# Retention, softplus and SwiGLU feed-forwards in one kernel: retention chunks 4 to 11 taken two at a time, with another order of tiles, conversions and loads around them

## The chip, the cores and the metric

One core of a Trainium2 chip runs the whole program. The metric is the device time of one execution in microseconds, as the median of a few runs.

## What is computed

Three stages follow each other: a multi-head retention (a linear attention whose state decays by a factor per head), a feed-forward layer with softplus, and a feed-forward layer with RMS norm and SwiGLU. Inputs are float32, and the weights reach the kernel as 64-bit numbers, which it converts itself.

```python
B, H, S, D = 2, 8, 768, 64                      # retention
for t in range(S):
    state = gamma * state + einsum('bhd,bhe->bhde', k[:, :, t], v[:, :, t])
    y[:, :, t] = scale * einsum('bhd,bhde->bhe', q[:, :, t], state)
x = y.transpose(0, 2, 1, 3).reshape(1536, 512)
h = x @ w_in                                    # 512 -> 2048
x = softplus(h) @ w_out                         # 2048 -> 512
xn = x / sqrt(mean(x * x) + 1e-6) * rms_g
out = (silu(xn @ w_gate) * (xn @ w_val)) @ w_out2   # 512 -> 1536 -> 512
```

## The kernel before

**Retention in chunks.** The 768 positions of each of the two batch rows are cut into 6 chunks of 128, so there are 12 chunks, 0 to 11; four of them make one block of 512 tokens, the tile `x[bi]` (blocks 0 to 2). One chunk takes these steps on TensorE, each for all 8 heads:

- `step_t` (L250 to L270): eight transposes `pt` of k and q. VectorE multiplies the turned q by a decay table into the tile `at` (L261), ScalarE copies the turned k into it (L266). Both must be there before the scores.
- `step_s`: products `sc` of turned k and q (L278). VectorE multiplies them by the masks (L280, two instructions of 128x512).
- `step_u`: products `u` of k and v (L291); GpSimd has scaled k first (`prep`, L248). VectorE adds `u` to the faded state (L297); GpSimd fades the state (`fade`, L302). The last chunk of a batch row, 5 and 11, has no such step.
- `step_y`: products `y` of state and q (L318; not in the first chunk of a batch row, 0 and 6), then of v and the masked scores into the same banks (L325). ScalarE writes a rounded high part into `x[bi]`, VectorE the rest (`split`, L119).

These products use parts of TensorE's array: `sc` has tiles of 64x128, `y` from the state 64x64, `y` from v and `u` 128x64; the transposes and all large products use the whole 128x128. The profile prints that shape behind the names.

**Large products.** `project` (L342) makes one tile `h` of the first layer from 12 matmuls of 512 columns: four pieces of the contraction for each of three products of high and low parts. `l2` (L378) makes the tiles `l` in the same way. `l1`'s `after()` is the softplus: Abs, Exp and Ln on ScalarE (L359 to L361), one VectorE instruction (L362), and later a split into `g`.

**Weights.** `load_weight` brings a tile of 512 KB into one of three stages, `convert` makes the float32 high and low parts: ScalarE `c` and `a` (L163, L164), VectorE `w` twice (L165, L167), GpSimd the sum `c` (L169), and from the list `deferred` VectorE `a` (L178, `finish`), ScalarE the high part and GpSimd the low part (L120, L121). The order on VectorE is the order in which the code issues.

**Order.** The schedule is written by hand: every engine runs its instructions in the order of the code and waits on semaphores. Chunks 0 to 3 run first (L552). Then, while block 0 and block 1 of the first layer are computed, each `h` tile is followed by one chunk (L579 to L608): the chunk's `y` and `u`, the scores of the next chunk, and the transposes of the chunk after the next one. So a chunk's transposes, scores and outputs lie about one `h` tile (and more) apart. After that only large products follow to the end. All loads go through SyncE's queue in the order of the code; the eight PSUM banks are handed out in turn by `bank`.

Of the kernel before, what the change touches and what calls it, by code (L numbers as in the profile page):

```python
# [26 lines left out]
def retention_softplus_swiglu(ctx: ExitStack, tc: tile.TileContext, q, k, v, w_in, w_out,  # L27
# [31 lines left out]
    def bank(name, keep=False):  # L59
        i = oldest.pop(0)  # L60
        (kept if keep else oldest).append(i)
        return ps.tile([P, N], F32, tag=f"ps{i}", name=name)
# [91 lines left out]
    def convert():  # L154
        i = pos["conv"]
        if i >= pos["load"] or not free:
# [6 lines left out]
        nc.scalar.activation(out=c, in_=lo32, func=AF.Copy, scale=2.0 ** -29)  # L163
        nc.scalar.activation(out=a, in_=hi32.bitcast(F32), func=AF.Abs)  # L164
        nc.vector.tensor_scalar(out=w, in0=hi32, scalar1=3, scalar2=0x3FFFFFF8,  # L165
                                op0=ALU.logical_shift_left, op1=ALU.bitwise_and)
        nc.vector.scalar_tensor_tensor(out=w, in0=hi32, scalar=0xC0000000, in1=w,  # L167
                                       op0=ALU.bitwise_and, op1=ALU.bitwise_or)
        nc.gpsimd.tensor_tensor(out=c, in0=w, in1=c, op=ALU.add)  # L169
# [12 lines left out]

        deferred.append(finish if order[i][0] in ("w_in", "w_out") else lambda: deferred.append(finish))
        ws[order[i]] = t
        left[order[i]] = NB
        pos["conv"] += 1
        return True
# [11 lines left out]

    def flush(loads=True, order=1):  # L200
        todo = deferred[::order]
        deferred.clear()
        for s in todo:
            s()
        if loads:
            load_weight()
# [65 lines left out]
    def step_s(g):  # L272
# [6 lines left out]
        for e in range(2):  # L279
            nc.vector.tensor_tensor(out=t[:, 2 + e], in0=sc[e], in1=mask[e], op=ALU.mult)  # L280

    def step_u(g):
        c = g % CPB
        _, kk, vv = [qkv[g].pop(i) for i in range(3)]
        if c == CPB - 1:
            return
        u = bank("u")[:, 0:NP * D].rearrange("p (j t) -> p j t", j=NP)
        for j in range(NP):
            for e in range(2):
                h = 2 * j + e  # L290
                nc.tensor.matmul(u[e * D:(e + 1) * D, j, :], lhsT=kk[:, h, :], rhs=vv[:, NP * e + j, :],  # L291
                                 start=True, stop=True, skip_group_check=True)
        new = state[(c + 1) % 2]
        if c == 0:
            nc.vector.tensor_copy(new, u)
        else:
            nc.vector.tensor_tensor(out=new, in0=u, in1=faded, op=ALU.add)  # L297
# [7 lines left out]
    def step_y(g):  # L305
        c = g % CPB
        bi, ci = divmod(g, CB)
        if ci == 0:
            x[bi] = x_p.tile([P, 2, KC, N], F32R, tag="x", name=f"x{bi}")


        ys = [bank("y")[:, 0:2 * P].rearrange("p (i t) -> p i t", i=2) for _ in range(2)]
        t = tr.pop(g)

        if c:
            for i in range(2):
                for e, h in ((0, 0), (1, 1), (0, 1), (1, 0)):
                    nc.tensor.matmul(ys[e][h * D:(h + 1) * D, i, :], lhsT=state[c % 2][e * D:(e + 1) * D, 2 * i + h, :],  # L318
                                     rhs=t[e * D:(e + 1) * D, 0, 2 * i + h, :], start=(i == 0), stop=False,
                                     skip_group_check=True)  # L320
        for e in range(2):
            for i in range(2):
                for h in range(2):
                    j = 2 * i + h
                    nc.tensor.matmul(ys[e][h * D:(h + 1) * D, i, :], lhsT=qkv[g][2][:, NP * e + j, :], rhs=t[:, 2 + e, j, :],  # L325
                                     start=(c == 0 and i == 0), stop=True, skip_group_check=True)
        sl = slice(ci * P, (ci + 1) * P)
        for e in range(2):
            k2 = slice(2 * e, 2 * e + 2)
            split(x[bi][:, 0, k2, sl], x[bi][:, 1, k2, sl], ys[e])  # L330
# [22 lines left out]
    def l1(b, f):  # L353
        h = bank("h")
        project(h, weight("w_in", f), x[b])

        def after():
            t = t_p.tile([P, N], F32, tag="t", name="t")
            nc.scalar.activation(out=t, in_=h, func=AF.Abs)  # L359
# [3 lines left out]
            split_later((b, f), t)  # L363
        return after

    def l2(b, gr, m):
        fs = range(gr * G1, (gr + 1) * G1)
        keep = b == 0
        if keep:
            if gr == 0:  # L370
                acc[b, m] = bank("l2", True)
            p = acc[b, m]
        else:
            p = bank("l2")
# [106 lines left out]
    def l4(b, gr, m, fs=None):  # L481
# [3 lines left out]
        if fs[0] == grp[0]:  # L485
            if keep:
                if gr == 0:
                    acc["o", b, m] = bank("l4", True)
# [63 lines left out]
    for g in range(CB):  # L552
        load_next(g + 2)
        load_weight()
        if g == CB - 1:
            nc.sync.dma_start(out=rg, in_=rms_g.rearrange("(k p) -> p k", p=P))
        step_y(g)
        step_u(g)
        if g < CB - 1:
            fade(g)  # L560
        step_s(g + 1)
        if g < CB - 1:
# [3 lines left out]
        flush(False)  # L566
        if g % 2:
            convert()

    pend = None  # L570
    for gr in range(NG1):
        for b in range(NB):
            l1s = [lambda f=f: l1(b, f) for f in range(gr * G1, (gr + 1) * G1)]
# [3 lines left out]
            if pend:  # L577
                l2s = [lambda m=m: l2(*pend, m) for m in range(KC)]
# [100 lines left out]
```

## Time and profile before

| what | value |
|---|---|
| median of 3 runs | 621.01 us (620.82 to 622.0) |
| the profiled execution: its own time | 621.34 us |
| the profiled execution: span of its instructions | 619.6 us |
| TensorE busy (PE) | 613.1 us, 99% of the span |
| VectorE (DVE), ScalarE (ACT), GpSimd (POOL) busy | 382.4, 320.9, 197.9 us |
| granted TensorE clock | 1.00 of full speed (2.4 GHz) in every stretch |
| retention chunks lie within | the first 83.2 us |

The span is 1.7 us shorter than the execution's own time. Busy PE says little by itself, because matmuls are pipelined: how close together they start is read from the timeline.

### The profile page before, as it was taken

The page shows a single profiled execution, that of the slowest core. Times are in us where ns is not written, and L with a number is a line of the kernel's source. Part 1 is how long each engine was busy: PE and PEld are TensorE (multiplying, and loading weights), DVE is VectorE, ACT ScalarE, POOL GpSimd, SP SyncE. Part 2 cuts the span into 40 slices and gives each one's busy share as a digit, 9 for nine tenths or more (in the row PEclk, how much of TensorE's full clock was granted, in tenths as well). Part 3 has the DMA queues.
Part 4 walks back from the last instruction along what each step waited for, and adds up shares of the span by engine and source line. Part 5 has one row for each costly group of instructions (what it writes and reads, how often), then busy time and mean ns, then how long its engine had stood idle before and what let it go on. Part 6 is the DMA issues. An engine that isn't in the chain of part 4 may idle for free.

```text
span 619.6 us, 8589 instructions
## 1 busy us (share of the span) xinstructions
PE 613.1 (99%) x3304; PEld 509.4 (82%) x3304; DVE 382.4 (62%) x588; ACT 320.9 (52%) x555; POOL 197.9 (32%) x162
## 2 busy tenths in 40 slices
PE   9999999999999999999999999999999999999997
PEld 8788888888888888888888888888888888888885
DVE  5799817777754776367689866536683466722332
ACT  3477538887765776487576446324342334411111
POOL 3456404445520543033024425304252134400000
PEclk9999999999999999999999999999999999999999
DMA  9999312333220332021023313212231113000102
GB/s 198 238 246 226 86 35 68 103 102 103 71 66 1 102 103 68 1 71 66 0 69 103 93 45 102 69 34 69 68 104 34 49 54 103 0 1 18 51 35 102
DMA packets 65560, 48.84 MB, mean 79 GB/s; under 512 B 39792, under 2 KB 60528, under 8 KB 65520
## 3 DMA queue, kind: packets, MB, share of 16 engines
q1 hardware_dynamic: 64320, 47.90, 27.8%
q8 instruction: 26, 0.43, 0.3%
q10 hardware_dynamic: 1200, 0.39, 0.3%
q14 instruction: 14, 0.11, 0.1%
HBM read 45.14 MB, written 3.15 MB: 78 GB/s over the span
## 4 chain that ended last, share of the span: by engine, by line
PE 98%; DMA 1%; DVE 0%; ACT 0%; issue 0%; SPq 0%
PE l L378 21%; PE h L342 21%; PE l L496 16%; PE h_w_gate L342 16%; PE h_w_val L342 16%; PE sc L278 2%; PE y L325 2%; PE pt L259 2%; PE y L318 1%; PE u L291 1%; DMA k<-in_k_dram 1%; PE busy L212 0%; PE ms L433 0%; PE root L449 0%; DVE at L280 0%; PE pt L234 0%
## 5 line engine op out<-in xcount | busy, mean ns | idle before, releaser
L169 POOL TENSOR_TENSOR c<-w,c 128x512 uint32<-128x512 uint32 x68 | 87.9, 1292 | 243.8 <-DVE w L167 209.0
L342 PE MATMUL h<-x,ws_w_in 128*128 128x512 f32 x576 | 139.2, 391 | 0.0
L378 PE MATMUL l<-g,ws_w_out 128*128 128x512 f32 x576 | 137.9, 390 | 0.0
L378 PEld LDWEIGHTS l<-g,ws_w_out 128*128 128x128 f32 x576 | 107.9, 188 | 22.6 <-issue 0.2
L342 PEld LDWEIGHTS h<-x,ws_w_in 128*128 128x128 f32 x576 | 107.6, 188 | 22.2
L120 ACT ACTIVATE g<-t 128x512 fp32r<-128x512 f32 x84 | 53.1, 632 | 109.4 <-DVE t L477 79.3
L342 PE MATMUL h_w_gate<-xn,ws_w_gate 128*128 128x512 f32 x432 | 104.0, 390 | 0.0
L342 PE MATMUL h_w_val<-xn,ws_w_val 128*128 128x512 f32 x432 | 103.9, 389 | 0.0
L496 PE MATMUL l<-ws_w_out,g 128*128 128x512 f32 x432 | 103.4, 389 | 0.0
L496 PEld LDWEIGHTS l<-ws_w_out,g 128*128 128x128 f32 x432 | 81.0, 188 | 16.8
L342 PEld LDWEIGHTS h_w_val<-xn,ws_w_val 128*128 128x128 f32 x432 | 81.0, 188 | 16.8
L342 PEld LDWEIGHTS h_w_gate<-xn,ws_w_gate 128*128 128x128 f32 x432 | 80.9, 188 | 16.7
L362 DVE SCALAR_TENSOR_TENSOR t<-h,t 128x512 f32<-128x512 f32 x48 | 33.2, 691 | 79.3 <-ACT t L361 79.2
L121 DVE TENSOR_TENSOR g<-t,g 128x512 fp32r<-128x512 f32 x84 | 62.1, 739 | 25.1 <-ACT g L120 21.6
L473 ACT ACTIVATE t<-t 128x512 f32<-128x512 f32 x36 | 22.8, 633 | 90.2 <-DVE t L472 90.2
L477 DVE TENSOR_TENSOR t<-h_w_val,t 128x512 f32<-128x512 f32 x36 | 24.8, 689 | 63.0 <-PE h_w_val L342 61.7
L178 DVE SCALAR_TENSOR_TENSOR a<-a,c 128x512 f32<-128x512 f32 x68 | 59.7, 879 | 3.8 <-POOL c L169 3.8
L359 ACT ACTIVATE t<-h 128x512 f32<-128x512 f32 x48 | 28.7, 597 | 47.8 <-PE h L342 47.7
L121 POOL TENSOR_TENSOR ws_w_out<-a,ws_w_out 128x512 fp32r<-128x512 f32 x28 | 36.2, 1294 | 40.1 <-ACT ws_w_out L120 40.1
L472 DVE TENSOR_TENSOR t<-h_w_gate,root 128x512 f32<-128x512 f32 x36 | 24.8, 688 | 25.6 <-PE h_w_gate L342 23.7
L121 POOL TENSOR_TENSOR ws_w_in<-a,ws_w_in 128x512 fp32r<-128x512 f32 x16 | 22.7, 1416 | 36.9 <-ACT ws_w_in L120 36.9
L361 ACT ACTIVATE t<-t 128x512 f32<-128x512 f32 x48 | 30.4, 633 | 1.5
(88 smaller groups left out, 578.7 us busy)
## 6 DMA issues: line engine op xcount, KB each, us to landing
st_w_out<-in_moe_w_out_dram SPq DMA_DIRECT2D x28, 512.0 KB, 3.3
st_w_in<-in_moe_w_in_dram SPq DMA_DIRECT2D x16, 512.0 KB, 3.8
st_w_gate<-in_moe_w_gate_dram SPq DMA_DIRECT2D x12, 512.0 KB, 3.5
st_w_val<-in_moe_w_val_dram SPq DMA_DIRECT2D x12, 512.0 KB, 3.5
v<-in_v_dram SPq DMA_DIRECT2D x12, 256.0 KB, 4.8
q<-in_q_dram SPq DMA_DIRECT2D x23, 128.0 KB, 4.5
k<-in_k_dram SPq DMA_DIRECT2D x23, 128.0 KB, 4.2
out_dram<-o SPq DMA_DIRECT2D x11, 256.0 KB, 2.0
```

Source lines behind the costliest of these rows:

```text
L120: nc.scalar.activation(out=hi, in_=src, func=AF.Copy)
L121: eng.tensor_tensor(out=lo, in0=src, in1=hi.bitcast(F32), op=ALU.subtract)
L169: nc.gpsimd.tensor_tensor(out=c, in0=w, in1=c, op=ALU.add)
L178: nc.vector.scalar_tensor_tensor(out=a, in0=a, scalar=TINY, in1=c.bitcast(F32), op0=ALU.is_ge, op1=ALU.mult)
L342: nc.tensor.matmul(h, lhsT=w[:, i, kk * P:(kk + 1) * P], rhs=src[:, j, kk, :], start=(n == 0), stop=(n == 3 * KC - 1))
L359: nc.scalar.activation(out=t, in_=h, func=AF.Abs)
L361: nc.scalar.activation(out=t, in_=t, func=AF.Ln, bias=1.0)
L362: nc.vector.scalar_tensor_tensor(out=t, in0=h, scalar=0.0, in1=t, op0=ALU.max, op1=ALU.add)
L378: nc.tensor.matmul(p, lhsT=w[:, i, m * P:(m + 1) * P], rhs=g_t[b, f][:, j, :], start=(n == 0 and f == (0 if keep else fs[0])), stop=(n == ...
L472: nc.vector.tensor_tensor(out=t, in0=h, in1=root[b], op=ALU.mult)
L477: nc.vector.tensor_tensor(out=t, in0=h, in1=t, op=ALU.mult)
L496: nc.tensor.matmul(p, lhsT=g_t[b, f][:, j, m * P:(m + 1) * P], rhs=w[:, i, :], start=(n == 0 and f == (0 if keep else grp[0])), stop=(n == ...
```

## The change

Chunks 4 to 11 are taken as the pairs (4, 5), (6, 7), (8, 9), (10, 11) in a new function `batch`. In a pair the transposes of both chunks stand together, then all scores, all `u`, the products from the state, and the products from v. `u` of both chunks shares one bank, and so do the two chunks' `y` (each split is now one instruction of 512 elements where there were two of 256). The steps of `convert` are issued apart from each other within the pair. Between the pairs stand one or two `h` tiles: one before (4, 5) and (6, 7), two before (8, 9) and (10, 11). The loads and conversions of the region are written out by hand.

```diff
+    def outputs(gs):
...
+        w = len(gs) * P
+        ys = [bank("y")[:, 0:2 * w].rearrange("p (i t) -> p i t", i=2) for _ in range(2)]
...
+        for n, g in enumerate(gs):
+            c = g % CPB
+            if c:
+                for i in range(2):
+                    for e, h in ((0, 0), (1, 1), (0, 1), (1, 0)):
+                        product(e, h, i, n, state[c % 2][e * D:(e + 1) * D, 2 * i + h, :],
+                                tr[g][e * D:(e + 1) * D, 0, 2 * i + h, :], False)
+        for n, g in enumerate(gs):
+            for e in range(2):
+                for i in range(2):
+                    for h in range(2):
+                        j = 2 * i + h
+                        product(e, h, i, n, qkv[g][2][:, NP * e + j, :], tr[g][:, 2 + e, j, :], True)
...
+    def batch(a, after, more=()):
+        gs = (a, a + 1)
+        after.size()
+        rest = take()
+        parts = convert(True)
+        if parts:
+            bits, small, total, size, finish = parts
+            bits()
+        if a not in tr:
+            step_t(a)
+        if parts:
+            small()
+        step_t(a + 1)
+        for g in gs:
+            prep(g)
+        if parts:
+            total()
+        scores(a)()
+        masked = scores(a + 1)
+        after()
+        if parts:
+            size()
+        adds = update(gs)
+        if adds:
+            adds.pop(0)()
+            fade(a)
+        masked()
+        parted = outputs(gs)
+        if adds:
+            adds.pop(0)()
+        todo = take()
+        for do in rest:
+            do()
+        if parts:
+            finish()
+        for do in todo:
+            do()
+        for do in take():
+            do()
+        parted()
...
+            elif (gr, b) == (0, 1):
+                after = first[0]()
...
+                batch(4, after)
...
+                batch(6, first[1]())
+                load(8, 2)
+                load(9, 2)
+                load_weight()
+                load(10, 0)
+                load(10, 1)
+                convert()
+                load_weight()
+                load(11, 0)
+                load(11, 1)
+                piece(first[2](), 1)
+                batch(8, l1s[0]())
+                load(10, 2)
+                load(11, 2)
+                piece(first[3](), 1)
+                batch(10, l1s[1]())
+                piece(l1s[2](), 0)
+                piece(l2s.pop(0)(), 0)
```

`bits` are the two VectorE instructions `w`, `small` and `size` the ScalarE ones, `total` GpSimd's sum, `finish` the VectorE instruction `a` with the splits behind it.

TensorE, one full chunk with the `h` tile ahead of it, before (chunk 8's outputs; `k_605` is chunk 8's k, `k_696` chunk 9's, `k_790` chunk 10's):

```order
L342 MATMUL h<-x_516,ws_w_in 128x512 x12
L318 MATMUL y<-at,state_116 64x128 x8
L325 MATMUL y<-at,v_699 64x128 x8
L291 MATMUL u<-v_699,k_605 64x64 x8
L278 MATMUL sc<-at 128x128 x8
```

TensorE, the pair (8, 9) with the two `h` tiles ahead of it, in the change (`k_585` and `q_582` are chunk 8's, `k_591` and `q_588` chunk 9's):

```order
L386 MATMUL h<-x_205,ws_w_in 128x512 x12
L386 MATMUL h<-x_531,ws_w_in 128x512 x12
L274 MATMUL pt<-ident,k_585 128x128 x4
L274 MATMUL pt<-ident,q_582 128x128 x4
L274 MATMUL pt<-ident,k_591 128x128 x4
L274 MATMUL pt<-ident,q_588 128x128 x4
L293 MATMUL sc<-at 128x128 x16
L314 MATMUL u<-v_730,k_585 64x64 x8
L314 MATMUL u<-v_732,k_591 64x64 x8
L346 MATMUL y<-at,state_116 64x128 x8
L346 MATMUL y<-at,state_117 64x128 x8
L346 MATMUL y<-at,v_730 64x128 x8
```

The transposes now stand directly ahead of the scores that read them, with no `h` tile between, and the state of the second chunk is needed eight products after `u`.

VectorE before, from one chunk's scores to the next one's (`a` and `w` belong to the conversion, `t` to the softplus, `g` to its split):

```order
L280 TENSOR_TENSOR at<-sc,mask 128x512 x2
L261 TENSOR_TENSOR at<-pt,tab 128x512
L178 SCALAR_TENSOR_TENSOR a<-a,c 128x512
L121 TENSOR_TENSOR g<-t,g 128x512
L362 SCALAR_TENSOR_TENSOR t<-h,t 128x512
```

VectorE in the change, between the outputs of the pair (6, 7) and the scores of the pair (8, 9):

```order
L187 SCALAR_TENSOR_TENSOR a<-a,c 128x512
L121 TENSOR_TENSOR g<-t,g 128x512
L121 TENSOR_TENSOR x_531<-y,x_531 128x2x256 x2
L171 TENSOR_SCALAR w<-st_w_in_578 128x512
L173 SCALAR_TENSOR_TENSOR w<-st_w_in_578,w 128x512
L187 SCALAR_TENSOR_TENSOR a<-a,c 128x512
L171 TENSOR_SCALAR w<-st_w_out_580 128x512
L173 SCALAR_TENSOR_TENSOR w<-st_w_out_580,w 128x512
L414 SCALAR_TENSOR_TENSOR t<-h,t 128x512
L171 TENSOR_SCALAR w<-st_w_out_734 128x512
L173 SCALAR_TENSOR_TENSOR w<-st_w_out_734,w 128x512
L276 TENSOR_TENSOR at<-pt,tab 128x512 x2
```

Three conversions (`w` three times) stand ahead of the decay multiply of chunk 8, and the middle `a` needs GpSimd's sum of the conversion just ahead of it.

SyncE's queue before, behind chunk 3's k (`v_201` is chunk 2's v, `q_257` and `k_260` are chunk 4's):

```order
L77 DMA v_201<-in_v_dram 128x8x64
L148 DMA st_w_in_203<-in_moe_w_in_dram 128x4x256
L80 DMA q_257<-in_q_dram 128x4x64 x2
L80 DMA k_260<-in_k_dram 128x4x64 x2
L77 DMA v_263<-in_v_dram 128x8x64
```

The same place in the change (`v_203` is chunk 2's v, `v_257` chunk 3's, `q_327` and `k_330` chunk 4's):

```order
L148 DMA st_w_in_201<-in_moe_w_in_dram 128x4x256
L77 DMA v_203<-in_v_dram 128x8x64
L77 DMA v_257<-in_v_dram 128x8x64
L80 DMA q_327<-in_q_dram 128x4x64 x2
L80 DMA k_330<-in_k_dram 128x4x64 x2
```

The first weight tile now goes ahead of chunk 2's v, and both v's ahead of chunk 4.

## Rows read from the trace of the kernel before

**Rows 1.** The page's first part: busy time, share of the span, instructions.
```profile
PE 613.1 (99%) x3304; PEld 509.4 (82%) x3304; DVE 382.4 (62%) x588; ACT 320.9 (52%) x555; POOL 197.9 (32%) x162
```
**Rows 2.** The page's chain that ended last, by engine.
```profile
PE 98%; DMA 1%; DVE 0%; ACT 0%; issue 0%; SPq 0%
```
**Rows 3.** Busy time by stretch, 40 to 60 us (columns: PE, PEld, DVE, ACT, POOL, clock, DMA, GB/s).
```profile
40.00:60.00 20.00, 20.00 (x236) 16.78 (x235) 19.78 (x33) 15.45 (x31) 13.05 (x12) 1.00 1.05 240
```
**Rows 4.** Timeline of PE, one chunk and its large tile (start us, length us, instruction).
```profile
49.16 0.67 PE L318 MATMUL y<-at,state 64*64 64x128 f32 x16
49.76 1.09 PE L325 MATMUL y<-at,v 128*64 128x128 f32 x16
50.68 0.63 PE L291 MATMUL u<-v,k 128*64 128x64 f32 x16
51.25 1.16 PE L278 MATMUL sc<-at 64*128 64x128 f32 x16
52.34 0.66 PE L259 MATMUL pt<-ident,k 128*128 128x128 f32 x4
52.83 0.60 PE L259 MATMUL pt<-ident,q 128*128 128x128 f32 x4
53.19 3.00 PE L342 MATMUL h<-x,ws_w_in 128*128 128x512 f32 x12
56.12 0.67 PE L318 MATMUL y<-at,state 64*64 64x128 f32 x16
```
**Rows 5.** Timeline of PE, neighbours of other kinds, 25 to 38 us.
```profile
25.54 3.03 PE L342 MATMUL h<-x,ws_w_in 128*128 128x512 f32 x12
28.41 0.60 PE L259 MATMUL pt<-ident,k 128*128 128x128 f32 x4
28.84 0.60 PE L259 MATMUL pt<-ident,q 128*128 128x128 f32 x4
...
36.92 1.09 PE L325 MATMUL y<-at,v 128*64 128x128 f32 x16
37.94 1.16 PE L278 MATMUL sc<-at 64*128 64x128 f32 x16
```
**Rows 6.** The chain in order of time: a large tile among large tiles.
```profile
91.66 2.72 PE l L378 x12
```
**Rows 7.** Timeline of PE, chunks 2 and 3 (in brackets: idle before, and what ended it).
```profile
17.64 1.09 PE L325 MATMUL y<-at,v 128*64 128x128 f32 x16
...
20.82 0.63 PE L259 MATMUL pt<-ident,k 128*128 128x128 f32 x4 [0.53 <-DMA k<-in_k_dram]
...
22.95 1.09 PE L325 MATMUL y<-at,v 128*64 128x128 f32 x16 [0.47 <-DVE at L280]
```
**Rows 8.** Timeline of ACT: the first conversion.
```profile
18.98 0.68 ACT L163 ACTIVATE c<-st_w_in 128x512 uint32<-128x512 uint32 x1 [1.62 <-DMA st_w_in<-in_moe_w_in_dram]
```
**Rows 9.** Timeline of DVE, 53 to 57 us.
```profile
53.02 0.41 DVE L297 TENSOR_TENSOR state<-u,faded 128x256 f32<-128x256 f32 x1
53.35 0.41 DVE L165 TENSOR_SCALAR w<-st_w_out 128x512 uint32<-128x512 uint32 x1
53.80 0.69 DVE L167 SCALAR_TENSOR_TENSOR w<-st_w_out,w 128x512 uint32<-128x512 uint32 x1
54.41 1.28 DVE L280 TENSOR_TENSOR at<-sc,mask 128x512 f32<-128x512 f32 x2
55.61 0.68 DVE L261 TENSOR_TENSOR at<-pt,tab 128x512 f32<-128x512 f32 x1
56.21 0.85 DVE L178 SCALAR_TENSOR_TENSOR a<-a,c 128x512 f32<-128x512 f32 x1
56.98 1.54 DVE L121 TENSOR_TENSOR g<-t,g 128x512 fp32r<-128x512 f32 x1
```
**Rows 10.** Timeline of POOL: the sum of the conversion of rows 9.
```profile
54.64 1.30 POOL L169 TENSOR_TENSOR c<-w,c 128x512 uint32<-128x512 uint32 x1 [1.55 <-DVE w L167]
```
**Rows 11.** A group of ACT's, 25 to 90 us: the weights' high part (busy us, mean ns).
```profile
L120 ACT ACTIVATE ws_w_in<-a 128x512 fp32r<-128x512 f32 x3 | 1.8, 613 | 0.0
```

More of the change, by code (lines that the diff above doesn't have):

```diff
@@ L57, in retention_softplus_swiglu, with bank @@
     oldest, kept = list(range(8)), []
[L59 removed]
+    def bank(name, to=oldest):
         i = oldest.pop(0)
[L61 removed]
+        to.append(i)
         return ps.tile([P, N], F32, tag=f"ps{i}", name=name)
@@ L186, in convert @@
         pos["conv"] += 1
+        if parts:
+            return bits, small, total, size, finish
+        for do in (small, size, bits, total):
+            do()
+        deferred.append(finish if order[i][0] in ("w_in", "w_out") else lambda: deferred.append(finish))
         return True
@@ L198, in weight, with take @@
         return ws[nm, f]
+    def take():
+        todo = deferred[:]
+        deferred.clear()
+        return todo
     def flush(loads=True, order=1):
-        todo = deferred[::order]
-        deferred.clear()
-        for s in todo:
+        for s in take()[::order]:
             s()
@@ L270, in step_t, with scores @@
         turned(g, order)
-    def step_s(g):
+    def scores(g):
         t = tr[g]
@@ L278, in step_s, with masked, update, added @@
                 nc.tensor.matmul(sc[e][:, j, :], lhsT=t[r, 1, j, :], rhs=t[r, 0, j, :], start=True, stop=True)
-        for e in range(2):
-            nc.vector.tensor_tensor(out=t[:, 2 + e], in0=sc[e], in1=mask[e], op=ALU.mult)
-    def step_u(g):
[L283 to L297, printed above, removed]
+        def masked():
+            for e in range(2):
+                nc.vector.tensor_tensor(out=t[:, 2 + e], in0=sc[e], in1=mask[e], op=ALU.mult)
+        return masked
+    def step_s(g):
+        scores(g)()
+    def update(gs):
+        u = bank("u").rearrange("p (g j t) -> p g j t", g=2, j=NP)
+        todo = []
+        for i, g in enumerate(gs):
+            c = g % CPB
+            kk, vv = qkv[g][1], qkv[g][2]
+            if c == CPB - 1:
+                continue
+            for j in range(NP):
+                for e in range(2):
+                    h = 2 * j + e
+                    nc.tensor.matmul(u[e * D:(e + 1) * D, i, j, :], lhsT=kk[:, h, :], rhs=vv[:, NP * e + j, :],
+                                     start=True, stop=True, skip_group_check=True)
+            def added(c=c, i=i):
+                new = state[(c + 1) % 2]
+                if c == 0:
+                    nc.vector.tensor_copy(new, u[:, i])
+                else:
+                    nc.vector.tensor_tensor(out=new, in0=u[:, i], in1=faded, op=ALU.add)
+            todo.append(added)
+        return todo
+    def step_u(g):
+        for do in update([g]):
+            do()
+        qkv.pop(g)
     def fade(g):
@@ L303, in fade @@
                                     op=ALU.mult)
-    def step_y(g):
-        c = g % CPB
-        bi, ci = divmod(g, CB)
+    def outputs(gs):
+        bi, ci = divmod(gs[0], CB)
         if ci == 0:
             x[bi] = x_p.tile([P, 2, KC, N], F32R, tag="x", name=f"x{bi}")
[L312 to L330, printed above, removed]
@@ new lines, in outputs, with parted @@
+        for n, g in enumerate(gs):
+            for e in range(2):
+                for i in range(2):
[3 more added lines that the diff above has]
+        for g in gs:
+            tr.pop(g)
+        sl = slice(ci * P, ci * P + w)
+        def parted():
+            for e in range(2):
+                k2 = slice(2 * e, 2 * e + 2)
+                split(x[bi][:, 0, k2, sl], x[bi][:, 1, k2, sl], ys[e])
@@ L363, in after @@
             split_later((b, f), t)
+        after.size = size
         return after
```

142 lines of the change are left out of this document (88 added, 54 removed).

## The prediction, made blind

> **What bounds the kernel now.** I read the page's busy times first, then the chain that ended last, then TensorE's timeline. TensorE is busy 99% of the span [rows 1], and 98% of the chain is TensorE [rows 2]. So a gain has to shorten TensorE's own stream, and a loss has to make it wait. The timeline tells which of its instructions are dearer than they need be. A large tile between large tiles takes 2.72 us [rows 6]. The same tile behind a chunk takes 53.19 to 56.12, which is 2.93 [rows 4]. So something is lost where the kinds of product meet. Then I looked at who would have to keep up: from 40 to 60 us VectorE is busy 19.78 of 20 us, while TensorE is busy all 20 [rows 3]. VectorE is thus nearly as full as TensorE there, and TensorE does not wait only because what VectorE must deliver is asked for late, a large tile after it was begun. The loads are full too: 240 GB/s with the 16 DMA engines marked over 100% busy [rows 3]. Everything behind the retention is a dense stream of large tiles, the same in both kernels, so a time gained or lost in the retention goes to the end unchanged.
>
> **What the pairing removes.** TensorE loses time wherever the shape of the array's tile changes. At the old end: `y` from v takes 49.76 to 50.68, 0.92 us, when `u` of the same shape follows [rows 4], and 36.92 to 37.94, 1.02, when the scores of another shape follow [rows 5]; that is 0.10. At the new end: the transposes of k take 52.34 to 52.83, 0.49, behind the scores [rows 4], and 28.41 to 28.84, 0.43, behind a large tile of their own shape [rows 5]; that is 0.06. So a change costs about 0.16. Into a large tile the new end is dearer: 25.54 to 28.41 is 2.87 against 2.72, 0.15 [rows 5, 6].
>
> A chunk before has four such changes (large tile to state products, to v products, `u` to scores, scores to transposes; from transposes to the large tile there is none). Two chunks have eight. A pair in the change has five: transposes to scores, scores to `u`, `u` to state products, these to v products, and v products to the large tile. Three fewer in each of four pairs is 12, and 12 x 0.16 = **-1.9 us**. The lower bound is the old end alone, 12 x 0.10 = 1.2. The upper is 12 x 0.25 = 3.0, if each were as dear as one into a large tile. Some of the changes (transposes to scores directly, scores to `u`, `u` to state products) stand nowhere in these rows, so I take the middle.
>
> The Trainium skill, "TensorEngine Tiling (Array Packing)", section Key Properties, says that another tiling mode drains TensorE; "TensorE: Matmul & The Clock Gate", Part 2, puts the drain at about 128 cycles. An estimate from that page is 0.053 us a change and 0.6 in all. The rows show two to three times that for one change, so they decide; by the page the sum below would be 1.3 us worse.
>
> **What the edits of little cost are.** Eight fewer splits of `x` on each of ScalarE and VectorE cost or save TensorE nothing by themselves: each is half as wide before. The banks and lists shift no work. The number of loads, conversions and large tiles up to the dense part is the same.
>
> **What the other order of loads adds.** In the change chunk 2's v stands behind the first weight tile. Before, TensorE began the products with that v at 17.64 without a wait [rows 7], and the weight tile behind it had landed by 18.98, when the waiting ScalarE began [rows 8]. The two together are the same bytes in one queue, so in the change v comes last, at about 18.98, and TensorE waits 18.98 - 17.64 = 1.35. Chunk 3's v products then wait for masked scores: VectorE has the conversion's `a` (0.68, when nothing holds it up) ahead of the masks, which begin 0.6 later than the scores allow. The products could begin about 22.15 and get the first mask about 22.55, the second 0.60 later; I take 0.45. The two waits of before, 0.53 for k and 0.47 for the mask [rows 7], go away. Together 1.35 + 0.45 - 1.0 = **+0.8**. If v still lands in time, it is -0.55; if the loads behind it slip as well, perhaps +2.
>
> **What the lost distance adds.** In a pair the scores follow directly on the transposes that feed them. VectorE must then be free at that moment, and it runs its list in order. Take the pair (8, 9). From the start of the conversion's `a` behind the pair (6, 7), VectorE and its suppliers need: `a` 0.68; the weight's high part on ScalarE 0.61 + 0.04; the first high part of `x` there 0.53; then on VectorE two low parts at 0.60 each; `w`, `w` at 0.45 and 0.69; GpSimd's sum 0.15 + 1.30; 0.27 until VectorE's `a` goes on; `a` 0.60; `w`, `w` 0.45 + 0.61; softplus `t` 0.60; `w`, `w` 0.45 + 0.61; the decay multiply 0.68 and 0.04 to TensorE. The lengths are those of [rows 9 to 11]: VectorE's next instruction starts 0.08 before the end of the last one (two masks in 1.28, so 0.60 each), the sum on GpSimd began 0.15 after the second `w`, and `a` 0.27 after its end; a split of 512 I take like the other instructions of that width. It adds up to 9.96 us.
>
> TensorE in the same time needs the high part of the weight (0.68 + 0.04 + 0.61 + 0.04 = 1.37), then two large tiles 2.87 + 2.72, four groups of transposes at 0.43 and 0.10 for the change: 8.78. So it waits **1.2** for the scores. The wait sits behind GpSimd's sum: there VectorE stands idle 1.7 us with a full list behind it. The pair (10, 11) has the same list with one conversion's turn less, but its softplus is queued on ScalarE behind a conversion: **1.0**.
>
> Two smaller kinds. The second chunk's state products need the state, which VectorE adds after `u`, 0.41 long [rows 9], and behind the softplus's `t`. In the pair (6, 7) nothing else stands between, so 0.55; in the others the first chunk's state products (0.45) cover most: 0.27, 0.08 and 0.27. Then the large tile behind the pair (6, 7) needs a weight's high part that waits for VectorE's `a`, queued behind the masks: 0.3. These are 1.5 together, and all waits in the pairs 1.2 + 1.0 + 1.5 = **+3.7**. The bounds: none, if VectorE is never behind; and, if each `a` and `g` is held up by GpSimd as the `g` of 1.54 beside 0.68 is [rows 9], 0.86 more in each of two pairs, 5.4.
>
> **Sum.** -1.9 + 0.8 + 3.7 = +2.6; as two of the waits overlap a change of shape that is already counted, 0.1 each, +2.4 to 2.6, and I take +2.5. The profiled execution had 621.34 us, 0.33 above the median of its kernel's runs, so 623.8 there and **623.5** as a median.
>
> **Rivals.**
> - *VectorE catches up.* What speaks for it: it has 0.2 us idle in 20 before [rows 3], two of its pairs now have two large tiles ahead, and its work shrinks a little. Against it: the order of its list, with GpSimd's sum in the middle, which no freedom of VectorE shortens. If the waits in the pairs come to 1.1 instead of 3.7, the sum is 0.0: 621.0.
> - *Faster: the changes of shape are the larger thing.* If VectorE's list is served before TensorE asks (the conversion's sum on GpSimd being done while the large tiles run), the waits in the pairs are 0.3 and chunk 2's v lands with the queue's next bytes, at half of the wait (0.1 in the sum). Then -1.9 + 0.1 + 0.3 = -1.5: 619.5. It decides where the two waits for scores stay under 0.3 each.
> - *GpSimd holds VectorE.* An `a` or `g`, both of whose inputs lie in SBUF, took 1.54 where GpSimd worked at the same time [rows 9]. If that falls on the lists of two pairs, 2 x 0.86 more: 625.2. The Trainium skill, "SBUF — State Buffer", section Who interferes with whom, says that such an instruction contends with a GpSimd instruction that reads SBUF; the row agrees.
> - *Loads come late.* Pairs want two chunks' loads at once while the queue is full [rows 3]. Chunk 5's k, moved ahead of several others, would have to be 2 us late to cost 1: 624.5. This I count with the one before.
>
> **How the numbers follow.** The forecast, slower by 1.3 to 3.9 us (622.3 to 624.9), has a chance of 0.59; VectorE catching up 0.18; faster 0.15; held up by GpSimd or loads 0.08. The predicted time is the first one's. The range goes from 620.5, in the case of VectorE catching up, to 625.4, in the last; outside of it I leave 0.13 below and 0.06 above. A difference under 0.2% (1.24 us) can't be told from none: faster than that (under 619.8) 0.15, the same 0.19, slower 0.66.
>
> **What would show it.** Right: in the profile of the changed kernel TensorE's timeline has idle time before the first `sc` of the pairs (8, 9) and (10, 11), about 1 us each, ended by VectorE's decay multiply; a wait of over 1 us before chunk 2's v products ended by the load of v; 0.2 to 0.6 before a second chunk's state products; and a pair without waits takes about 0.5 less than two chunks did. The dense part then runs as before. Wrong: those brackets are missing or under 0.3, or the pair's products are not closer together than the single chunks' were, or a wait stands behind the retention, where I expect none.

## The result, and the profile after

The changed kernel takes **629.0 us** (median of 4 runs, 627.87 to 630.81) against 621.01 before: ratio 1.0128, 95% interval 1.0096 to 1.016. I forecast 623.5, 620.5 to 625.4. The sign is right, the size is not. The profiled execution has 630.11 us and a span of 628.4, which is 8.8 more than the 619.6 before. The four runs differ by 2.9 us (two took 627.87 and 627.88), and what follows is the account of the profiled one.

The page's busy times (first part), TensorE's granted clock in 40 slices of the span, and the chain by engine, to be read beside [rows 1, 2]:

```profile
PE 614.5 (98%) x3304; PEld 511.3 (81%) x3304; DVE 384.5 (61%) x580; ACT 321.3 (51%) x547; POOL 198.1 (32%) x162
...
PEclk9997999999999999999999999999999999999999
...
PE 92%; DVE 3%; DMA 3%; ACT 2%; issue 0%; SPq 0%; DVEq 0%; ACTq 0%
```

TensorE has 1.4 us more busy time for the same instructions, its chain has other engines in 8% of the span, and in one slice its clock isn't full. The busy times by stretch (columns as in [rows 3]: PE, PEld, DVE, ACT, POOL, clock, DMA, GB/s):

```profile
40.00:60.00 20.00, 15.69 (x178) 13.78 (x178) 14.30 (x24) 13.11 (x24) 10.38 (x10) 0.89 1.02 249
57.00:61.00 4.00, 3.75 (x34) 3.55 (x34) 2.37 (x5) 1.26 (x3) 0.93 (x1) 0.50 1.24 231
```

From 40 to 60 us VectorE is busy 14.30 of 20 us, where it had 19.78 [rows 3], so it stands idle itself while TensorE waits. From 57 to 61 the granted clock is 0.50, which is 1.2 GHz instead of 2.4. TensorE's timeline, in the places that answer to [rows 4, 5, 7]:

```profile
18.94 1.09 PE L346 MATMUL y<-at,v 128*64 128x128 f32 x16 [0.84 <-DMA v<-in_v_dram]
...
22.50 1.25 PE L346 MATMUL y<-at,v 128*64 128x128 f32 x16 [0.31 <-DVE at L297]
...
24.99 2.99 PE L386 MATMUL h<-x,ws_w_in 128*128 128x512 f32 x12
...
43.41 0.67 PE L346 MATMUL y<-at,state 64*64 64x128 f32 x16 [0.53 <-DVE state L320]
...
46.19 5.75 PE L386 MATMUL h<-x,ws_w_in 128*128 128x512 f32 x24 [0.22 <-ACT ws_w_in L120]
...
53.09 0.60 PE L274 MATMUL pt<-ident,q 128*128 128x128 f32 x4
57.26 3.78 PE L293 MATMUL sc<-at 64*128 64x128 f32 x32 [3.57 <-ACT a L168]
60.97 1.88 PE L314 MATMUL u<-v,k 128*64 128x64 f32 x32
62.78 1.27 PE L346 MATMUL y<-at,state 64*64 64x128 f32 x32
...
75.19 2.06 PE L293 MATMUL sc<-at 64*128 64x128 f32 x32 [1.78 <-DVE at L276]
...
100.29 2.88 PE L431 MATMUL l<-g,ws_w_out 128*128 128x512 f32 x12
```

The last row is the fifth `l` tile. Before, it began at 91.50, so the whole 8.8 us is lost ahead of it; the dense part runs as before. The two rows of before that this and the lead-in are read from:

```profile
24.44 1.16 PE L278 MATMUL sc<-at 64*128 64x128 f32 x16
...
91.50 2.88 PE L378 MATMUL l<-g,ws_w_out 128*128 128x512 f32 x12
```

The 8.8 consist of four things:

- **Lead-in, +0.55.** The first large tile begins at 24.99. Before, it began at 25.54 [rows 5], but with the scores of chunk 4 already done (24.44 to 25.54, 1.10), so at 24.44 like for like.
- **Waits in the pairs, +6.7.** Scores of (8, 9) 3.57 and of (10, 11) 1.78; 0.53 and 0.22 around the pair (6, 7); and three small ones of 0.2 each (transposes and state products of the pair (4, 5), state products of (10, 11)).
- **Half clock, +2.5.** Scores of a pair take 1.98 from start to start elsewhere, here 57.26 to 60.97, 3.71; `u` takes 1.81 where 1.08 is usual.
- **Pairing, -0.9.** That is what is left: 8.8 - 0.55 - 6.7 - 2.5.

Who was late for the 3.57? The row names ScalarE, but the scores need VectorE's decay multiply, `at`, which began at 56.43, its first half ending just ahead of 57.26. VectorE's timeline, beside [rows 9]:

```profile
51.64 0.69 DVE L173 SCALAR_TENSOR_TENSOR w<-st_w_out,w 128x512 uint32<-128x512 uint32 x1
52.25 0.68 DVE L414 SCALAR_TENSOR_TENSOR t<-h,t 128x512 f32<-128x512 f32 x1
54.28 0.77 DVE L171 TENSOR_SCALAR w<-st_w_out 128x512 uint32<-128x512 uint32 x1 [1.35 <-DMA st_w_out<-in_moe_w_out_dram]
55.08 1.43 DVE L173 SCALAR_TENSOR_TENSOR w<-st_w_out,w 128x512 uint32<-128x512 uint32 x1
56.43 1.27 DVE L276 TENSOR_TENSOR at<-pt,tab 128x512 f32<-128x512 f32 x2
```

The transposes were done at about 53.7. In front of the decay multiply stands the conversion's `w`, which waits 1.35 for a weight tile and then takes 0.77 and 1.43 where it took 0.41 and 0.69 [rows 9]. The tile, in the chain in order of time (start, and length from issue to landing):

```profile
48.52 5.74 DMA st_w_out<-in_moe_w_out_dram
```

### The profile page after: what moved, and what is told of

It reads as the page before. It is cut to its first block, busy times and chain, and to the rows that moved or that the text cites. A ratio compares the mean times of both kernels' runs of the same rounds, so it can differ in the third digit from the quotient of the medians.

```text
span 628.4 us, 8558 instructions
## 1 busy us (share of the span) xinstructions
PE 614.5 (98%) x3304; PEld 511.3 (81%) x3304; DVE 384.5 (61%) x580; ACT 321.3 (51%) x547; POOL 198.1 (32%) x162
## 4 chain that ended last, share of the span: by engine, by line
PE 92%; DVE 3%; DMA 3%; ACT 2%; issue 0%; SPq 0%; DVEq 0%; ACTq 0%
PE l L431 21%; PE h L386 19%; PE l L549 16%; PE h_w_gate L386 16%; PE h_w_val L386 16%; PE sc L293 2%; PE y L346 1%; PE pt L274 1%; DMA v<-in_v_dram 1%; DMA st_w_out<-in_moe_w_out_dram 1%; DVE at L297 1%; DMA k<-in_k_dram 1%; PE u L314 1%; DVE a L187 0%; PE ms L486 0%
## 5 line engine op out<-in xcount | busy, mean ns | idle before, releaser
L187 DVE SCALAR_TENSOR_TENSOR a<-a,c 128x512 f32<-128x512 f32 x68 | 58.1, 855 | 5.2 <-POOL c L177 5.2
L121 POOL TENSOR_TENSOR ws_w_out<-a,ws_w_out 128x512 fp32r<-128x512 f32 x28 | 37.7, 1350 | 41.8 <-ACT ws_w_out L120 41.8
```

The source lines that it names most:

```text
L121: eng.tensor_tensor(out=lo, in0=src, in1=hi.bitcast(F32), op=ALU.subtract)
L187: nc.vector.scalar_tensor_tensor(out=a, in0=a, scalar=TINY, in1=c.bitcast(F32), op0=ALU.is_ge, op1=ALU.mult)
```

## The experiments

Each was timed beside the kernel before on the same chip; the ratio is to that kernel, whose median was 621.55 to 621.89 there. Theory A: VectorE's in-order list, held up by a late load, makes the scores wait, and TensorE's idleness costs it its clock. The rivals stand in the expectations.

**The weight tile first.** In the code behind the pair (6, 7):

```diff
                 batch(6, first[1]())
+                load_weight()
                 load(8, 2)
                 load(9, 2)
-                load_weight()
```

> One part of the change moved: behind the pair (6, 7) the weight tile that VectorE and ScalarE waited for at 54.28 us is loaded ahead of the v of chunks 8 and 9, not behind them. Theory A (the load comes late, VectorE's list stands still behind it, TensorE waits 3.6 us for the scores of (8, 9), and the idle TensorE is then granted half its clock): the list starts about 1 us earlier, the wait for the scores of (8, 9) falls from 3.6 to 1.5 to 2.8 us; if the clock still falls the median is 627 to 628, if it stays at 1.00 it is 624 to 626. Rival B (the list of conversions itself is too long, the load hides nothing): the wait stays at 3.3 to 3.7 us, 629. Rival C (the clock falls because the products of a pair stand together, whatever the wait): the scores of (8, 9) still take 3.7 us.

627.19 us, ratio 1.0087 (1.0074 to 1.01). TensorE and VectorE:

```profile
56.34 2.06 PE L293 MATMUL sc<-at 64*128 64x128 f32 x32 [2.53 <-DVE at L276]
...
52.92 1.20 DVE L171 TENSOR_SCALAR w<-st_w_out 128x512 uint32<-128x512 uint32 x1
54.16 1.43 DVE L173 SCALAR_TENSOR_TENSOR w<-st_w_out,w 128x512 uint32<-128x512 uint32 x1
```

In this profile the wait for the load is gone, and with it 1.04 of the 3.57. 2.53 are left without it, so the list itself (rival B) is the larger part. That the new place of the load did it is not shown: two runs below leave that load where the change has it, and their profiles have no wait for it either. The clock stayed at 1.00, and the scores take 2.06 although a pair's products stand together: rival C is out. The median misses the 624 to 626 expected for a full clock; two of the four runs have a mean granted clock of 0.997 and took 627.65 and 627.96, the other two 1.000 and 626.72 and 626.18. Slow `w` beside GpSimd stands out as a cause that I had not named for this place:

```profile
52.55 1.29 POOL L177 TENSOR_TENSOR c<-w,c 128x512 uint32<-128x512 uint32 x1 [1.93 <-DMA v<-in_v_dram]
53.79 2.71 POOL L263 TENSOR_TENSOR k<-k,dec 128x512 f32<-128x512 f32 x2
```

**GpSimd's k behind its sum**, on top of that run:

```diff
-        for g in gs:
-            prep(g)
         if parts:
             total()
+        for g in gs:
+            prep(g)
```

> On top of the run with the weight tile first (627.2 us; waits of 2.53 and 1.79 us for the scores of (8, 9) and (10, 11)): GpSimd scales the k of a pair behind its sum, not ahead of it, so that it doesn't work beside VectorE's two w. In that run the two w took 1.20 and 1.43 us beside GpSimd's k, and 0.42 and 0.69 elsewhere. Theory D (GpSimd slows VectorE's two w, which are ahead of the decay multiply): w and w take 0.45 and 0.69, the waits fall by 0.9 to 1.4 us to about 1.2 to 1.5 and 0.6 to 0.9, 625.0 to 625.8. Rival (w is slow for the fresh transfer or for another reason): w stays at 1.2 and 1.4, the waits stay, 627.

626.62 us, ratio 1.0082 (1.0069 to 1.0095). TensorE, then VectorE:

```profile
56.64 2.06 PE L293 MATMUL sc<-at 64*128 64x128 f32 x32 [1.79 <-DVE at L276]
...
53.96 1.20 DVE L171 TENSOR_SCALAR w<-st_w_out 128x512 uint32<-128x512 uint32 x1
55.20 0.69 DVE L173 SCALAR_TENSOR_TENSOR w<-st_w_out,w 128x512 uint32<-128x512 uint32 x1
```

The second `w` fell from 1.43 to 0.69 and the wait by 0.74; at (10, 11) from 1.79 to 1.08. The first `w` still runs beside another GpSimd instruction (the sum of the conversion before, 53.59 to 54.88) and still takes 1.20. So theory D holds, a little short of the expected size. The time hardly fell (the two waits give 1.45, the medians 0.6, the two ratios are not clear of each other), since `u` now waits for k: 0.71, 0.31 and 0.33 in the first two pairs.

**`w` behind the decay multiplies.**

```diff
             bits, small, total, size, finish = parts
-            bits()
...
             prep(g)
         if parts:
+            bits()
             total()
```

> One part of the change moved: in each pair VectorE's two instructions w of the conversion stand behind the decay multiplies instead of ahead of them, so that the scores no longer queue behind them. Theory A (in-order list behind a late load): the wait for the scores of (8, 9) falls from 3.6 us to under 1.0 and that of (10, 11) from 1.8 to under 0.5, the granted clock stays at 1.00, the scores of (8, 9) take 2.0 us instead of 3.7; together 3.6 + 1.8 + 2.5 less about 1.5 that is left or comes back at the masks: 622 to 624. Rival B (what holds the decay multiply is work ahead of the conversion, softplus and the parts of x): the waits fall by under a third, 627 to 629. Rival C (the clock falls through the closeness of the small products): the waits fall but the scores still take 3.7 us, 625 to 626.

624.69 us, ratio 1.0048 (1.0036 to 1.006). Both waits for scores are gone and the clock stays full; about half of it comes back one step later, at the state:

```profile
54.40 2.06 PE L293 MATMUL sc<-at 64*128 64x128 f32 x32
...
59.40 0.67 PE L346 MATMUL y<-at,state 64*64 64x128 f32 x16 [1.27 <-DVE state L322]
```

State waits of 0.71, 0.91, 1.27 and 0.70 in the four pairs: my "about 1.5 that is left" was too small.

**The idle time filled.**

```diff
+        if a == 8:
+            keep_busy(14)
         scores(a)()
```

> Added work: 14 matmuls on constants (their results are not used) ahead of the scores of (8, 9), which fill some 3 us in which TensorE waited. The wait is not shortened by it. Theory A (the clock falls to half because TensorE stood idle): the granted clock stays at 1.00 behind it, the scores take 2.0 us instead of 3.7 and u 1.1 instead of 1.8, so 2.5 us are won although work was added: 626 to 627. Rival C (the clock falls through the mix of small products): the scores still take 3.7 us, 629 to 630.

626.94 us, ratio 1.0085 (1.0072 to 1.0098), though work was added. TensorE, then VectorE:

```profile
53.32 3.29 PE L227 MATMUL busy<-ones 128*128 128x128 f32 x28
56.54 2.06 PE L293 MATMUL sc<-at 64*128 64x128 f32 x32
...
52.65 1.21 DVE L171 TENSOR_SCALAR w<-st_w_out 128x512 uint32<-128x512 uint32 x1
55.25 1.27 DVE L276 TENSOR_TENSOR at<-pt,tab 128x512 f32<-128x512 f32 x2
```

The scores take 2.06 and the clock is 1.00. But this profile alone does not show that the filling did it. With the loads in the same order as in the change, the weight tile was in time here: issued at 47.79, it landed 4.3 us later, and `w` began at 52.65 without a wait. The first half of the decay multiply ended at about 55.9, so TensorE would have waited only some 2.6 us, and behind 2.53 the clock stayed full with nothing filled in. What speaks for idleness is all five runs together: their mean granted clocks are 0.999 to 1.000, those of the changed kernel's four runs 0.992 to 0.997.

The tile's lateness thus belongs to the execution that was profiled; that its place in the queue makes it late is not shown.

**A longer wait elsewhere**, on top of the run with the weight tile first:

```diff
+        if a == 10:
+            for _ in range(6):
+                nc.vector.tensor_copy(idle, mask[0])
         if a not in tr:
             step_t(a)
```

> On top of the run with the weight tile first (627.2 us, no stretch at half clock): six copies of a mask to an unused tile, added to VectorE's list ahead of the decay multiplies of the pair (10, 11). Their results are not used. They lengthen the wait for these scores from 1.79 us to 4 or 5. Theory A (TensorE's idleness of some 3.5 us or more lowers its granted clock): the clock behind it is 0.5, the scores of (10, 11) take 3.7 us instead of 2.06 and what follows is slower too, so that the time grows by the added wait and about 2 to 2.5 us on top: 631 to 633. Rival (the clock fell in the pair (8, 9) for a reason of that place): the scores take 2.06 us, and the time grows by the added wait alone, 629.5 to 630.5.

632.86 us, ratio 1.0177 (1.016 to 1.0194).

```profile
75.00 3.59 PE L293 MATMUL sc<-at 64*128 64x128 f32 x32 [5.40 <-DVE at L276]
78.52 0.69 PE L314 MATMUL u<-v,k 128*64 128x64 f32 x16
```

These scores took 2.06 in the same place without the copies, so the longer wait lowered the clock. From 75 to 78 us the granted clock is 0.50, and `u` is back at full speed. From start to start the scores take 3.52 instead of 1.98, which is 1.5 lost. Against the run without the copies the median is 5.7 higher, for 3.6 of added wait; the profiled run is the shortest of the four (631.26, mean clock 0.996), and what the others (0.991 to 0.993) lost beyond it no trace shows. In the profiled executions the clock stayed full behind waits of 1.78 to 2.58 and fell behind 3.57 and 5.40. Runs without a trace keep it open whether it can fall behind the shorter ones too: two of four with the weight tile first have a mean clock of 0.997.

**Chunk 2's v first**, as before:

```diff
-            load_weight()
             load(2, 2)
+            load_weight()
```

> One part of the change undone: in the first chunks the v of chunk 2 is loaded ahead of the first weight tile again, as before. If the lead-in's cost is the load behind which v stands (theory A): the wait of 0.9 us ahead of chunk 2's products with v goes away, the first large tile starts 0.3 to 0.9 us earlier than 24.99, and as the waits in the pairs stay, 628.1 to 628.7. Rival: what is behind the weight tile in the queue comes later by the same, the wait reappears at chunk 3 or in the pairs: 629.

626.99 us, ratio 1.0091 (1.0075 to 1.0107). In the lead-in the rival is right. The wait for v is gone and two others take its place, since VectorE's and ScalarE's conversion now starts later and stands ahead of chunk 2's state:

```profile
21.17 0.67 PE L346 MATMUL y<-at,state 64*64 64x128 f32 x16 [0.81 <-DVE state L322]
22.41 1.25 PE L346 MATMUL y<-at,v 128*64 128x128 f32 x16 [0.58 <-DVE at L297]
```

The first large tile begins at 24.91 instead of 24.99; the profiles of the runs above, with the load order of the change, have 24.63 to 24.99, so nothing is won. The median is 2 us lower all the same, but not by the lead-in: in its profile the wait for the scores of (8, 9) is 2.57 and the clock stays full, since the weight tile behind the pair (6, 7), which was not moved, came in time. Three of the six runs have mean clocks of 0.994 to 0.997 and took 627.48 to 629.81.

**Transposes one tile earlier** (the distance restored in two pairs):

```diff
...
                 piece(first[2](), 1)
+                step_t(8)
+                step_t(9)
                 batch(8, l1s[0]())
...
                 piece(first[3](), 1)
+                step_t(10)
+                step_t(11)
                 batch(10, l1s[1]())
```

> One part of the change undone: the transposes of the pairs (8, 9) and (10, 11) stand one large tile earlier, ahead of the second of the two h tiles, so that there is again a large tile between transposes and scores. Theory A (the scores wait because the decay multiply comes late in VectorE's list, and the distance of a tile hides that): the waits for the scores of both pairs are under 0.3 us and the granted clock stays at 1.00; a wait of 0.5 to 1.3 us ahead of the state products takes their place, since VectorE's list is no shorter. The change's 629.0 less 3.6, 1.8 and 2.5, plus 1.2 to 2: 622.5 to 624. Rival (the work, not its place, is too much for VectorE): the same wait of 3 us comes back at the masks, 626 to 628.

623.42 us, ratio 1.0032 (1.002 to 1.0043). As theory A has it: no wait for scores, 1.31 and 0.34 for the state, since `w`, slow beside GpSimd, still stands ahead of the masks.

**The pair served first on VectorE**, in (8, 9) and (10, 11):

```diff
-            bits()
+            if a < 8:
+                bits()
...
-        if parts:
+        if parts and a < 8:
             total()
         scores(a)()
         masked = scores(a + 1)
-        after()
-        if parts:
-            size()
+        if a < 8:
+            after()
+            if parts:
+                size()
         adds = update(gs)
...
         if adds:
             adds.pop(0)()
+        if a >= 8:
+            after()
+            if parts:
+                size()
+                bits()
+                total()
         todo = take()
```

> Another order on VectorE in the pairs (8, 9) and (10, 11) alone: the decay multiplies, the masks and the state additions first, then softplus, the two w and GpSimd's sum. The transposes stay where the change has them. Theory A (order of VectorE's list): no wait over 0.3 us for the scores, nor for the state (1.27 and 0.70 us in the run with w behind the decay multiplies), 622.3 to 623.3. Rival (the conversions were ahead for a reason): a large tile behind the pairs waits 1 to 3 us for its weights or for its g, 624 to 627.

626.04 us, ratio 1.0071 (1.0059 to 1.0084): the rival. The pair (8, 9) has no wait at all, and the tile behind it pays; the scores of (10, 11) still wait 0.87, and an `l` tile 0.63 for its weight. TensorE:

```profile
45.93 5.78 PE L386 MATMUL h<-x,ws_w_in 128*128 128x512 f32 x24 [0.22 <-ACT ws_w_in L120]
51.55 0.60 PE L274 MATMUL pt<-ident,k 128*128 128x128 f32 x4
...
52.86 0.60 PE L274 MATMUL pt<-ident,q 128*128 128x128 f32 x4
53.46 2.06 PE L293 MATMUL sc<-at 64*128 64x128 f32 x32
55.45 1.15 PE L314 MATMUL u<-v,k 128*64 128x64 f32 x32
56.53 1.27 PE L346 MATMUL y<-at,state 64*64 64x128 f32 x32
57.73 1.97 PE L346 MATMUL y<-at,v 128*64 128x128 f32 x32
59.62 2.10 PE L386 MATMUL h<-x,ws_w_in 128*128 128x512 f32 x8
63.73 3.93 PE L386 MATMUL h<-x,ws_w_in 128*128 128x512 f32 x16 [2.00 <-POOL ws_w_in L121]
```

What was deferred ahead of the pair (GpSimd's low part of a weight) now stood behind the new sum. These rows also show the pair by itself. With its two large tiles it takes 45.93 to 59.62, 13.69. Two chunks and two large tiles took 13.91 before: from 53.19 [rows 4] to this row of the kernel before:

```profile
67.10 3.00 PE L342 MATMUL h<-x,ws_w_in 128*128 128x512 f32 x12
```

So pairing wins **0.22** in this pair, and 0.9 in four if the others win as much. The 0.9 left over in the sum of the 8.8 agrees.

**All waits taken out**, in three steps on top of the early transposes. First: VectorE's masks and state additions first, then what was deferred, then softplus and `w`; in the lead-in the state addition and masks ahead of the split of `x`; both `h` tiles ahead of the four `l` tiles. The core of it (`first` is true in these two pairs):

```diff
-        after()
-        if parts:
-            size()
         adds = update(gs)
         if adds:
             adds.pop(0)()
             fade(a)
-        masked()
+        if first:
+            masked()
...
+        if first:
+            after()
+            if parts:
+                size()
+                bits()
+                total()
+                deferred.append(finish)
```

> A version that tries to keep the pairs and take the waits away, on top of the run with early transposes (623.4 us, span 621.7). In the pairs (8, 9) and (10, 11) VectorE's masks and state additions stand ahead of the softplus and the conversion's w, with what was deferred before the pair between them. In the other pairs the first state addition stands ahead of the softplus, and the weight's last steps ahead of the second. In the first chunks chunk 2's v is loaded ahead of the weight tile, and the state addition and the masks stand ahead of the split of x and of the conversion. At the end both h tiles stand ahead of the four l tiles. Theory A (the order of VectorE's list is what the pairs cost, and their products alone are 0.2 us a pair shorter than two single chunks): the waits of 1.3, 0.3, 0.5 and 0.2 us go, the first large tile starts 0.8 to 1.2 us earlier, span 618 to 619, median 619.5 to 621. Rival (VectorE is full, so that what is served late makes a later tile wait): a wait of 1 to 2 us at a large tile for its weights or its g, median 621 to 623.

623.76 us, ratio 1.0032 (1.0021 to 1.0044). That is above both expectations. The state waits of (8, 9) and (10, 11) went; new ones came:

```profile
25.82 2.12 PE L386 MATMUL h<-x,ws_w_in 128*128 128x512 f32 x8 [0.91 <-DVE x L121]
...
69.05 2.06 PE L293 MATMUL sc<-at 64*128 64x128 f32 x32 [1.24 <-DVE at L276]
```

Second, the core of it:

```diff
         adds = update(gs)
+        if parts and not first:
+            size()
+            if a == 6:
+                finish()
         if adds:
             adds.pop(0)()
...
         masked()
+        if not first:
+            after()
...
-                piece(first[3](), 1)
+                after = first[3]()
                 step_t(10)
                 step_t(11)
+                piece(after, 1)
```

> The run before (623.8 us, span 622.1) showed which waits its order made or left: 0.91 us in the first large tile for VectorE's part of x behind a state addition that waits for GpSimd, 0.48 and 0.49 ahead of two h tiles for a weight's high part behind the masks, 0.53 for the state of chunk 7, 1.24 for the scores of (10, 11) behind a conversion. Here chunk 3's x is split ahead of its state addition, a weight's a stands ahead of the masks of the second chunk and the softplus behind them, the products of v of chunk 6 stand ahead of the state products of chunk 7, and the decay multiplies of (8, 9) and (10, 11) ahead of the conversion that is between. Theory A (the order of VectorE's list is what the pairs cost): these waits are each under 0.2 us, no new one is over 0.5, span 618.3 to 619.3, median 619.8 to 621.0, about 1 us better than the kernel before at best. Rival (VectorE is full there and gives the time back): the waits return at the l tiles or at a later h, 622 to 624.

623.74 us, ratio 1.0037 (1.0023 to 1.0051): every wait that it was written against is gone, and the largest new one is at `u` of the last pair, for GpSimd (0.15 and 0.33 more at `u` of (8, 9), and 0.36 and 0.55 for loads of k in the lead-in):

```profile
70.26 0.69 PE L314 MATMUL u<-v,k 128*64 128x64 f32 x16 [2.08 <-POOL k L263]
```

Third, GpSimd's k ahead of that sum:

```diff
                 step_t(10)
+                prep(10)
                 step_t(11)
+                prep(11)
```

> On top of the run before (623.7 us, span 621.3): GpSimd scales the k of the pairs (8, 9) and (10, 11) right behind their transposes, ahead of the sum of the conversion that stands between. In the run before, k was queued behind that sum, which waits for VectorE's w, and the products u waited 0.15, 0.33 and 2.08 us for it. Theory A: these waits go, nothing takes their place, span 618.6 to 619.4, median 620.3 to 621.2; against the kernel before that is a ratio of 0.998 to 1.000. Rival (VectorE and GpSimd are full, so the time comes back): a wait of over 1 us at the masks, the state or an l tile, 622.5 to 623.7.

**620.48 us** (11 runs) against 621.87, ratio **0.9982** (0.9973 to 0.9991), span 619.0. It beats the changed kernel. Against the one before the interval stays under 1, but the gain is smaller than the 0.2% that I had set as the least I can tell from none. From 40 to 60 us nothing waits; the second row is the first large tile:

```profile
40.00:60.00 20.00, 20.00 (x274) 17.00 (x271) 18.73 (x30) 13.34 (x24) 10.30 (x10) 1.00 0.93 229
...
23.60 3.00 PE L392 MATMUL h<-x,ws_w_in 128*128 128x512 f32 x12
```

0.65 for a k in the pair (4, 5) and 0.55 for a state in (10, 11) are left. Not all of the gain is the pairs': the first large tile begins at 23.60, against 24.44 like for like before, so the lead-in gives 0.84, and its steps need no pairs. With 0.9 from the pairs, less the 1.2 of the two waits, that is 0.54 of the 0.6 by which the spans differ. Single chunks with this lead-in were not run.

## Why the prediction was wrong

- **"What the lost distance adds" failed, in the wait for the scores of (8, 9).** The place, the engine and the reason (the order of VectorE's list) were right, and the runs that change only that order or that distance remove the wait. The size was 1.2 and is 3.57. The difference is 1.04 for a weight tile that lands late in the profiled execution (in two other runs it was in time from the same place in the queue, and the wait is some 2.6), 0.74 for `w` beside GpSimd's scaling of k, and about 0.8 for the first `w` beside GpSimd's sum (1.20 against 0.42; no run moves that sum alone, but where the pair was served first, with GpSimd idle, that `w` takes 0.42). Without the three some 1.0 is left, near the 1.2 of the sum. At (10, 11) 1.0 was forecast, 1.78 measured, and 1.08 without k beside `w`.
- **Both extras were on the list as small rivals, in other places.** I priced GpSimd on `a` and `g`, because [rows 9] show it there, and didn't ask what GpSimd does while `w` runs in the new order: `prep` of two chunks now stands just there. And I priced late loads at one k, not at the tile at the head of VectorE's list, where 1.04 of a wait of 1.35 reached TensorE.
- **A whole term was missing: the clock, +2.5.** No row of before shows TensorE idle for long in its stream, so nothing there priced it. The lengthened wait shows that the idleness did it; the five runs with the wait filled agree by their mean clocks.
- **What the pairing removes** was mis-sized: -1.9, measured -0.9. That is 0.075 for each of the 12 changes where I took 0.16 from single places. The changes do not add up, because some of what a new neighbour saves comes back at the next one: ahead of a large tile q's transposes take 0.36 [rows 4], ahead of scores 0.60. Of the 0.49 that scores (0.19), `u` (0.06) and two large tiles (0.24) gain in the undisturbed pair against two chunks of [rows 4], the transposes (0.21) and the other products (0.06) give 0.27 back.
- **What the other order of loads adds** was near in size: +0.8 forecast, +0.55 measured, with the waits where I foresaw them (0.84 for v, 1.35 forecast; 0.31 for the masks, 0.45 forecast). The cause was not: with the load order undone, other waits take their place and the first large tile begins no earlier. In these runs it begins earlier, at 23.60 to 24.35, only where VectorE's order in the lead-in was changed as well. So that the size came out near is in part luck.
- **The smaller waits** were right: 0.53 before the state products of the pair (6, 7) (0.55 forecast), 0.22 for the tile behind it (0.3), 0.2 in two others (0.27).
- The sum by the measured terms, 0.55 + 6.7 + 2.5 - 0.9, is the 8.8 of the profiled executions; the medians differ by 8.0.

## What to carry to other kernels

Where work is moved closer to what feeds it, read the in-order list of the feeding engine from its last free moment on, and ask of each entry what it waits for and who runs beside it on GpSimd; a late load at the head of that list is paid for the most part (1.04 of 1.35 here). Before a late load is put down to the order of the queue, look at a second execution of that order. Price an idle TensorE at more than its idle time once a wait is longer than any the trace already holds. And a saving found between neighbours has to be counted over the whole new sequence: a shape change that is dropped may have hidden something.

## What was not expected of the hardware

- VectorE's two `w` of 128x512 take 0.42 and 0.69 us alone, and up to 1.20 and 1.43 beside a GpSimd instruction that reads SBUF; moving GpSimd's away restores the second to 0.69. The Trainium skill, "SBUF — State Buffer", section Who interferes with whom, says that both kinds of instruction can contend with GpSimd; the runs agree.
- TensorE's granted clock went from 1.00 to 0.50 (2.4 to 1.2 GHz) behind waits of 3.57 and 5.40 us, and cost 2.5 and 1.5 us; behind waits up to 2.58 it did not in any profiled execution. Whether it sometimes does is open: runs without a trace, two of four with the weight tile first, three of six with chunk 2's v first and three of five of the second step to take the waits out, have mean clocks of 0.994 to 0.997, and most are 1 us or more longer than the runs beside them.
- The same weight load, 3.3 us in the median of its kind, took 5.74 from issue to landing in the changed kernel and 4.3 in the run with the wait filled, with the same loads ahead of it in the queue.
